# Attention and a gated two-layer product on one core: seven block products for eight in four chunks of tokens where there were two

## The chip, the core and the metric

The kernel runs on one NeuronCore of one Trainium2 chip. The core has five engines, each with an instruction queue of its own: TensorE (PE, matmuls; its weight loads are PEld), VectorE (DVE), ScalarE (ACT), GpSimd (POOL) and SyncE (SP, which here only issues DMA transfers). ACT issues a few transfers too. The metric is the device time of one execution in microseconds.

## What is computed

From the reference, with B = 8 batches, H = 8 heads, S = 576 positions, D = 64, and then 4608 tokens of 512 features and 2048 hidden units:

```python
q_d = q.reshape(B, H, Sd, factor, D).mean(axis=3)        # factor = 4; k_d, v_d alike
out_d = sm_attn(q_d, k_d, v_d)                            # softmax attention over 144 pooled positions
out_up = np.repeat(out_d, factor, axis=2)
mask = np.abs(pos[:, None] - pos[None, :]) < factor       # a band of 7 positions
scores = np.where(mask, scale * q @ k.T, -1e9)
out_local = softmax(scores) @ v
x = (out_up + out_local), heads side by side: 4608 x 512
h = x @ w_in                                              # GEMM1, 512 -> 2048
g = h * np.clip(h + 3.0, 0.0, 6.0) / 6.0
out = g @ w_out                                           # GEMM2, 2048 -> 512
```

All in fp32. The two GEMMs run in a rounded fp32 format: each operand is split into a high and a low part, and one product is three matmuls (high by high, high by low, low by high).

## The kernel before, in words

**Tokens and tiles.** The 4608 tokens are nine chunks of 512 (`PART`). One chunk's GEMM1 is 16 blocks `f` of 128 hidden units, each 4 x 3 matmuls of 128x512 into a PSUM bank `h0` or `h1` (line 1067). ACT takes relu of a block out of the bank (line 1073), DVE gates it (line 1077), ACT rounds the gated block to its high part (line 1081), DVE or POOL makes the low part (line 1085), and GEMM2 adds 4 x 3 matmuls of the block into the banks `o0` to `o3` (line 1126). At a chunk's end these four are evicted (lines 1015, 1017) and stored (line 1021).

**Attention units.** A unit is a batch and a pair of heads: 32 units, four to a batch. Batches 0 and 1 use PE for their transposes and run before and in chunk 0. For the 24 units of batches 2 to 7, PE sees one burst per unit: pooled scores and banded scores of the new unit (lines 501, 709) and the products with V of the unit that came two bursts earlier (lines 752, 664). Between them the unit's probabilities go to DRAM and come back rearranged (`put_d`, `get_d`, `put`, `get`: lines 608 to 643), and DVE transposes them in blocks of 32 (lines 631, 650). q and k come as 128-byte pieces and are transposed by DVE (lines 323, 329). The unit's result is added into `xt`, x transposed, which stays in SBUF until its chunk's split into high and low part (`plan_split`, lines 122 and 969).

**The last pair.** Chunks 7 and 8 are taken together (`plan_strassen`). Their 1024 tokens by 512 features, and two blocks of the input weights, are 2x2 block matrices, and seven products of half the depth (p1 to p7, six matmuls each, line 1370) take the place of eight. One group of seven is 42 matmuls and makes two blocks `f` for both chunks; there are eight groups. The token side needs seven matrices: b11, b21, b22 as they are and t1 to t4 as differences (line 1263), each split into high and low (line 1241). They lie where GEMM1 weights and the split x lay that no one reads any more. The weight side needs sums (lines 1333 to 1357). Products p1, p6, p7, p5 add into one bank, the "chain", which ACT copies out after p1, p6 and p7 (line 1386) before the next may add into it. The first chunk's GEMM2 runs between the products of the next group, the second chunk's GEMM2 after the last group (line 1460), from gated blocks that wait in SBUF. Twelve weight blocks are written to DRAM beforehand (line 1178) and read back (line 1321).

**What sets the order.** The program is written by a planner: each operation has costs, predecessors, buffers that it takes and frees and a latest time, and `Plan.emit` plays the kernel through and writes the instructions of each engine in the order of that play. Buffers are named slots at written-out addresses (`_slots`); most are given in a fixed turn (`ORDERED`). At run time each engine works its queue strictly in that order.

## Time and profile before

| | before |
|---|---|
| median of three runs (lowest to highest) | 905.93 us (903.33 to 907.97) |
| the profiled execution, own time | 904.18 us |
| its span, first to last instruction | 902.0 us |
| PE busy | 883.8 us (98%) |
| DVE, ACT, POOL busy | 592.2, 472.5, 237.5 us |
| DMA moved | 106.08 MB |

A row of the page's groups names the line, the engine, the operation, output <- input tiles, shape and count, then busy time, the mean of one instruction, and the idle time before the group with what ended it. The view by windows gives busy time of each engine in a stretch; DMA there is the mean busy share of the 16 DMA engines. The view in order of time gives start, length, and in brackets the idle time before an instruction. Matmuls overlap, so the length of one (0.39 us) is longer than the distance between two.

### The profile page before, as it was taken

The page shows a single profiled execution, that of the slowest core. Times are in us where ns is not written, and L with a number is a line of the kernel's source. Part 1 is how long each engine was busy: PE and PEld are TensorE (multiplying, and loading weights), DVE is VectorE, ACT ScalarE, POOL GpSimd, SP SyncE. Part 2 cuts the span into 40 slices and gives each one's busy share as a digit, 9 for nine tenths or more (in the row PEclk, how much of TensorE's full clock was granted, in tenths as well). Part 3 has the DMA queues.
Part 4 walks back from the last instruction along what each step waited for, and adds up shares of the span by engine and source line. Part 5 has one row for each costly group of instructions (what it writes and reads, how often), then busy time and mean ns, then how long its engine had stood idle before and what let it go on. Part 6 is the DMA issues. An engine that isn't in the chain of part 4 may idle for free.

```text
span 902.0 us, 19402 instructions
## 1 busy us (share of the span) xinstructions
PE 883.8 (98%) x6961; PEld 722.2 (80%) x6961; DVE 592.2 (66%) x1073; ACT 472.5 (52%) x1511; POOL 237.5 (26%) x316
## 2 busy tenths in 40 slices
PE   6999999999999999999999999999999999999997
PEld 5667788788888888888888888888888888888886
DVE  7898876466776766656666665666655868766422
ACT  5798866455655455555454535455552334444421
POOL 3655542044522132123211330223110222000000
PEclk9999999999999999999999999999999999999999
DMA  9999843366666663655365546777541022210011
GB/s 227 276 236 235 193 125 70 94 123 120 125 130 125 133 134 72 131 111 114 80 144 103 108 88 136 196 174 190 134 112 36 1 78 86 70 70 24 13 36 47
DMA packets 315759, 106.08 MB, mean 118 GB/s; under 512 B 251792, under 2 KB 298000, under 8 KB 315664
## 3 DMA queue, kind: packets, MB, share of 16 engines
q1 hardware_dynamic: 314384, 103.09, 49.7%
q10 hardware_dynamic: 1280, 1.76, 0.6%
q8 instruction: 55, 0.90, 0.4%
q14 instruction: 40, 0.33, 0.1%
HBM read 75.89 MB, written 28.90 MB: 116 GB/s over the span
## 4 chain that ended last, share of the span: by engine, by line
PE 90%; DMA 3%; DVE 2%; SPq 2%; ACT 1%; issue 0%; POOL 0%; ACTq 0%; DVEq 0%
PE o L1126 33%; PE h L1067 31%; PE o L1460 5%; PE a L1370 5%; PE h L1370 4%; PE a L1460 2%; PE h L1460 2%; PE a L709 2%; PE h L752 2%; PE a L501 1%; PE h L664 1%; DMA early<-in_v_dram 1%; DMA arena<-in_k_dram 1%; DMA out_dram<-arena 1%; SPq L323 0%; DMA arena<-in_q_dram 0%
## 5 line engine op out<-in xcount | busy, mean ns | idle before, releaser
L1126 PE MATMUL o<-wp,rounded 128*128 128x512 f32 x1344 | 324.1, 393 | 2.7 <-DVE arena L1017 1.6
L1067 PE MATMUL h<-rounded,wp 128*128 128x512 f32 x1344 | 316.9, 390 | 1.2 <-DVE arena L1077 1.0
L1067 PEld LDWEIGHTS h<-rounded,wp 128*128 128x128 f32 x1344 | 251.3, 188 | 54.8 <-DVE arena L1077 1.4
L1126 PEld LDWEIGHTS o<-wp,rounded 128*128 128x128 f32 x1344 | 249.5, 188 | 56.8 <-DVE arena L1017 2.0
L1077 DVE SCALAR_TENSOR_TENSOR arena<-arena,h 128x512 f32<-128x512 f32 x112 | 76.0, 679 | 61.8 <-ACT arena L1073 61.3
L1085 DVE TENSOR_TENSOR rounded<-arena,rounded 128x512 fp32r<-128x512 f32 x85 | 61.9, 730 | 72.0 <-PE o L1126 54.2
L1073 ACT ACTIVATE arena<-h 128x512 f32<-128x512 f32 x112 | 66.6, 594 | 78.8 <-PE h L1067 76.2
L1081 ACT CAST rounded<-arena 128x512 fp32r<-128x512 f32 x112 | 68.9, 615 | 73.9 <-PE o L1126 44.1
L565 ACT ACTIVATE arena<-arena 128x64 f32<-128x64 f32 x240 | 80.2, 337 | 0.5
L422 POOL TENSOR_TENSOR arena<-arena 32x256 f32<-32x256 f32 (+1 forms) x26 | 22.3, 858 | 117.0 <-DMA arena<-in_v_dram 116.9
L1085 POOL TENSOR_TENSOR rounded<-arena,rounded 128x512 fp32r<-128x512 f32 x27 | 35.9, 1331 | 63.9 <-PE o L1126 45.1
L329 DVE STREAM_TRANSPOSE arena<-arena 128x576 f32<-128x576 f32 x56 | 43.2, 771 | 12.7 <-DMA arena<-in_q_dram 6.3
L1460 PE MATMUL o<-wp,rounded 128*128 128x512 f32 x192 | 49.2, 389 | 0.0
L378 POOL TENSOR_TENSOR arena<-arena 128x144 f32<-128x144 f32 x33 | 14.9, 450 | 128.2 <-DVE arena L329 50.0
L565 ACT ACTIVATION_READ_ACCUMULATOR arena<-arena 128x1 f32 x240 | 45.2, 188 | 0.0
L1460 PEld LDWEIGHTS o<-wp,rounded 128*128 128x128 f32 x192 | 36.0, 188 | 7.5
L684 ACT ACTIVATE arena<-h 128x144 f32<-128x144 f32 x24 | 7.0, 290 | 66.2 <-PE h L664 66.2
L380 POOL TENSOR_TENSOR arena<-arena 128x144 f32<-128x144 f32 x66 | 38.7, 586 | 5.2
L541 ACT ACTIVATE arena<-arena 128x1 f32<-128x1 f32 (+1 forms) x78 | 15.0, 193 | 43.5 <-DVE arena L554 43.4
L1370 PE MATMUL a<-wp,wp 128*128 128x512 f32 x150 | 37.2, 389 | 0.0
L1446 DVE TENSOR_TENSOR rounded<-arena,rounded 128x512 fp32r<-128x512 f32 x27 | 18.6, 690 | 26.8 <-PE h L1460 21.1
L420 DVE TENSOR_REDUCE arena<-arena 128x128 f32<-128x512 f32 (+1 forms) x26 | 27.6, 1065 | 12.9 <-PE h L664 10.8
(240 smaller groups left out, 1239.9 us busy)
## 6 DMA issues: line engine op xcount, KB each, us to landing
rawp<-in_w_in_dram SPq DMA_DIRECT2D x16, 512.0 KB
rawp<-in_w_out_dram SPq DMA_DIRECT2D x16, 512.0 KB
arena<-in_q_dram SPq DMA_DIRECT2D x112, 72.0 KB
arena<-in_k_dram SPq DMA_DIRECT2D x112, 72.0 KB
pl<-arena SPq DMA_DIRECT2D x24, 320.0 KB
arena<-pl SPq DMA_DIRECT2D x96, 80.0 KB
arena<-in_v_dram SPq DMA_DIRECT2D x28, 256.0 KB
out_dram<-arena SPq DMA_DIRECT2D x89, 72.0 KB
```

The source lines that it names most:

```text
L329: nc.vector.transpose(out=qk[kind], in_=qk[kind])
L380: eng.tensor_tensor(t, t, x[:, :, r], op=ALU.add)
L420: eng.tensor_reduce(out=vd, in_=raw.rearrange("p r e -> p e r"), op=ALU.add, axis=AX.X)
L565: nc.scalar.activation(x[:, j], x[:, j], AF.Exp, bias=m[:, j:j + 1], scale=0.125, accum_out=s[:, j:j + 1])
L1067: nc.tensor.matmul(st["ps"], win[f][:, wt, kk * P:(kk + 1) * P], xs[part][:, kk], start=(kk == 0 and i == 0), stop=(kk == NK - 1 and i == ...
L1073: nc.scalar.activation(st["t"], st["ps"], AF.Relu, bias=3.0)
L1077: nc.vector.scalar_tensor_tensor(out=t, in0=t, scalar=6.0, in1=st["ps"], op0=ALU.min, op1=ALU.mult)
L1081: nc.scalar.copy(st["gh"], st["t"])
L1085: eng.tensor_tensor(st["gl"], st["t"], st["gh"].bitcast(F32), op=ALU.subtract)
L1126: nc.tensor.matmul(otile[n, m], gt[:, ms], wout[f][:, wt], start=(f == 0 and i == 0), stop=(f == NF - 1 and i == 2),)
L1370: nc.tensor.matmul(ps, weight(i, j, wt, kk), xpart(MOVING[j], part)[:, kk], start=first and kk == 0 and x == 0, stop=kk == half - 1 and x ...
L1460: nc.tensor.matmul(otile[n + t, m], gt[:, ms], wout[f][:, wt], start=f == 0 and x == 0, stop=f == NF - 1 and x == 2)
```

## The change

- `PAIRS = (5, 7)`: chunks 5 and 6 are a pair with seven products as well; chunks 0 to 4 stay as they were. The first pair's second GEMM2 is followed by the second pair, whose first products stand among it.
- **x by DRAM.** From batch `VIA = 2` on, a unit's x is added into one small buffer and written to DRAM by ACT's queue (`put_x`); the split of chunks 2 to 4 and the token matrices of the pairs are loaded from there (`load`, `load_x`) into the place of their own low part.
- **Gated blocks by DRAM.** In both pairs the second chunk's 16 gated blocks go to DRAM (`put_g`) and come back (`get_g`), two to three blocks ahead of their use. Both chunks of a pair now use the banks `o0` to `o3`.
- **Weights.** All 16 blocks of input weights are written to DRAM during and after chunk 0 (there were 12, around chunk 6), and 28 are read back.
- **Attention ahead.** Batches 2 to 6 must be done before the first pair starts. `due_of` gives latest times of their own, the products with V stand three bursts behind (`DEPTH`), and buffers get second places in the space that x left. q and k of two units come in one set of four transfers (`plan_qk`), the pooled probabilities in five transfers (there were eight), the tail of V in one (there were two).
- **Rules of the planner.** Operations off PE from chunk 2 on are sorted 50 us ahead (`AHEAD_BY`); a GEMM1 block gives way to a burst that waits for both `h` banks (`firm`, `yields`).

On PE, at the start of the first pair, before (a_8256 is the chain, h_8318 and h_8342 the banks of p4 and p3; one product is four to six rows, of which the first show here; "..." leaves the rest of it out):

```order
L1370 MATMUL a_8256<-wp_1213,wp_937 128x512
L1370 MATMUL a_8256<-wp_1237,wp_937 128x512
...
L1370 MATMUL h_8318<-wp_1428,wp_668 128x512
...
L1370 MATMUL a_8256<-wp_1306,wp_937 128x512
...
L1370 MATMUL h_8342<-rounded,wp_937 128x512 x2
...
L1370 MATMUL a_8256<-rounded,wp_937 128x512 x2
```

and of the change (h_6933 is the chain, first p6, then p7 from wp_1432 and p5 from wp_1205; h_7017 is p4, h_7043 p3; o_5870 is chunk 4's GEMM2):

```order
L1394 MATMUL h_6933<-rounded,wp_927 128x512 x2
...
L1173 MATMUL o_5870<-wp_1796,rounded 128x512 x3
L1394 MATMUL h_6933<-wp_1432,wp_927 128x512
L1394 MATMUL h_6933<-wp_1488,wp_927 128x512
...
L1394 MATMUL h_6933<-wp_1205,wp_927 128x512
L1394 MATMUL h_6933<-wp_1227,wp_927 128x512
...
L1394 MATMUL h_7017<-wp_1295,wp_736 128x512
...
L1394 MATMUL h_7043<-rounded,wp_927 128x512 x2
```

Before, a product into another bank stands between any two of the chain; in the change three matmuls stand between p6 and p7, and none between p7 and p5.

On ACT, at the same place of the change (L1409 copies the chain after p1, p6 and p7, L120 rounds t3, b22 and t4, L563 to L573 are a unit's softmax, L1061 evicts chunk 4's output):

```order
L1409 COPY arena<-h_6933 128x512
L563 ACTIVATE arena<-arena 128x1
L569 ACTIVATE first,arena<-a_6819,arena 128x144
L573 ACTIVATE arena<-arena 128x1
L120 CAST wp_1432<-arena 128x1024
L120 CAST rounded<-rounded 128x1024
L1409 COPY first<-h_6933 128x512
L120 CAST wp_1295<-arena 128x1024
L1061 ACTIVATE arena<-o_5797 128x512
L1061 ACTIVATE arena<-o_5870 128x512
L1409 COPY first<-h_6933 128x512
```

The rounding of t4 (wp_1295) now stands behind the copy of p6, so p4 cannot start before it.

On SP, one unit's transfers, before:

```order
L643 DMA arena<-pl_0_3840 32x20x32 x4
L616 DMA arena<-pd_0_3835 32x12x32 x4
L621 DMA arena<-pd_0_3835 32x3x16 x4
L397 DMA arena<-in_v_dram 64x4x128
L401 DMA arena<-in_v_dram 64x128
L608 DMA pd_1_4031<-arena 64x3x144 x2
L323 DMA arena<-in_q_dram 32x18x32 x4
L323 DMA arena<-in_k_dram 32x18x32 x4
L635 DMA pl_1_4077<-arena 128x5x128
```

and of the change:

```order
L638 DMA arena<-pd_1_4748 32x12x32 x5
L431 DMA arena<-in_v_dram 128x512
L435 DMA arena<-in_v_dram 32x512
L660 DMA arena<-pl_1_4873 32x20x32 x4
L422 DMA arena<-in_v_dram 64x4x128
L426 DMA arena<-in_v_dram 64x128
L630 DMA pd_2_5001<-arena 64x3x144 x2
L652 DMA pl_2_5093<-arena 128x5x128
L422 DMA arena<-in_v_dram 64x5x128
L292 DMA arena<-in_k_dram 32x36x32 x4
```

q or k of two units is now one row of four transfers, and the pooled probabilities one row of five.

The diff, cut to what the prediction speaks of:

```diff
+        if VIA <= b < WITHIN:
+            plan_qk(pair, un2, row0)
...
+        deep = DEPTH[new["un"] >= (VIA + 1, DEPTH[0])] if new else 0
+        old = next(units[0]) if len(units) >= max(deep, 1) else None
...
+    def plan_qk(pair, un, row0):
+        def get(t, kind):
+            pair[kind] = buf("qd", (kind, un), [P, 2, S])
+            raw = pair[kind].rearrange("p u (j i) -> p (u j) i", i=32)
+            for e in range(4):
+                nc.sync.dma_start(raw[32 * e:32 * e + 32], bass.AP(..., ap=[[ROW, 32], [32 * ROW, 2 * S // 32], [1, 32]]))
...
+            if b >= VIA:
+                if g == 0:
+                    st["xu"] = buf("xu", un, [P, S])
+                add_to(st["xu"][:, g * HALF:(g + 1) * HALF], g, 0, HALF)
+                return
...
+        def put_x():
+            if b not in xd:
+                xd[b] = dram.tile([P, NHP, S], F32, name=f"xd{b}", tag=f"xd{b}")
+            QUEUE[AWAY[2]](nc).dma_start(xd[b][:, hp], st["xu"])
...
+        def load(b, s0, off, cnt, k):
+            nc.sync.dma_start(part(1, k, off, cnt).bitcast(F32), xd[b][:, k:k + ks, s0:s0 + cnt])
...
+                via = [op("SP", 0.5, partial(load, b, s0, off, cnt, k), [x for h in range(k, k + ks) for x in x_done[b, h]] + gone,
+                          size=dma(P * ks, cnt * 4))] if b >= VIA else []
...
+        def load_x(name, t, kh):
+            def get(off, cnt):
+                b, s0 = divmod((n + t) * TOK + off, S)
+                nc.sync.dma_start(whole_x(name)[:, :, off:off + cnt], xd[b][:, kh * half:(kh + 1) * half, s0:s0 + cnt])
...
+        l11, l21, l12, l22 = (load_x(*x) for x in (("t1", 0, 0), ("t4", 0, 1), ("t3", 1, 0), ("t2", 1, 1)))
+        d1 = minus_x("t1", "t3", "t1", l12 + l11)
+        d2 = minus_x("t2", "t2", "t1", l22 + d1)
+        s2_ = split("t2", d2)
+        l22 = load_x("b22", 1, 1)
+        d3 = minus_x("t3", "b22", "t3", l22 + d1)
...
+                    def put_g(f=f, name=name):
+                        gs[1, f]["d"] = dram.tile([P, TOK], F32, name=f"gd{n}_{f}", tag=f"gd{n}_{f}")
+                        nc.sync.dma_start(gs[1, f]["d"], st[name])
...
+            def get_g():
+                g["t"] = {g["name"]: buf(*g["tok"], [P, TOK])}
+                nc.sync.dma_start(g["t"][g["name"]], g["d"])
...
-PAIR0, SPILL_AT, GROUP = 7, 5, 15.0
+PAIRS, GROUP = (5, 7), 15.0
+VIA, WITHIN, LATER = 2, 7, 100.0
+DUE = 170.0, 17.0, 248.0, 16.5
+SPILL_AT = 0
-DEPTH = 2
+DEPTH = 2, 3
+URGENT, AHEAD_BY = 2, 50.0
+AWAY = "SP", "SP", "ACT", "SP"
```

464 lines of the change are left out of this document (244 added, 220 removed).

## The prediction

> **What bounds the kernel now.** The page's first part and its chain of waits come first:
>
> ```profile
> PE 883.8 (98%) x6961; PEld 722.2 (80%) x6961; DVE 592.2 (66%) x1073; ACT 472.5 (52%) x1511; POOL 237.5 (26%) x316
> PE 90%; DMA 3%; DVE 2%; SPq 2%; ACT 1%; issue 0%; POOL 0%; ACTq 0%; DVEq 0%
> ```
>
> PE is busy nearly throughout and makes 90% of the chain. A busy PE need not run at its peak, so I read the distance between matmuls from the view in order of time, in chunk 8's last stretch before the pair:
>
> ```profile
> 711.55 5.60 PE L1126 MATMUL o<-wp,rounded 128*128 128x512 f32 x24
> 716.99 5.60 PE L1067 MATMUL h<-rounded,wp 128*128 128x512 f32 x24
> 722.43 5.60 PE L1126 MATMUL o<-wp,rounded 128*128 128x512 f32 x24
> 727.87 1.52 PE L1370 MATMUL a<-wp,wp 128*128 128x512 f32 x6
> ```
>
> 24 matmuls take 5.44 us from start to start, three times over: 0.2267 us each, with nothing lost between groups. The windows then say how full the rest is:
>
> ```profile
> 350.00:550.00 200.00, 200.00 (x1663) 165.95 (x1662) 126.11 (x240) 105.45 (x414) 46.34 (x76) 1.00 0.53 109
> 550.00:650.00 100.00, 100.00 (x833) 82.95 (x832) 63.36 (x121) 53.38 (x205) 21.70 (x36) 1.00 0.70 173
> 0.00:100.00 100.00, 88.84 (x990) 66.56 (x991) 86.27 (x174) 80.05 (x185) 54.40 (x61) 1.00 0.96 243
> L1067 PE MATMUL h<-rounded,wp 128*128 128x512 f32 x409 | 95.6, 389 | 0.0
> L1126 PE MATMUL o<-wp,rounded 128*128 128x512 f32 x390 | 93.5, 392 | 0.0
> L709 PE MATMUL a<-arena 64*64 64x64 f32 x320 | 7.9, 222 | 0.0
> ```
>
> A window's columns are PE, PEld, DVE, ACT, POOL, clock, DMA share and GB/s; the last three rows are PE's groups in 350 to 550. There, 799 big matmuls and 8 bursts (320 / 40) fill the 200 us: 799 x 0.2267 = 181.1, and 18.9 us for 8 bursts, 2.36 each. So a matmul taken out of this kernel is worth 0.2267 us for as long as the other engines, DMA and SP keep up. The granted clock is 1.00.
>
> **The sum, part by part.**
>
> *Products removed.* The order lists 3408 matmuls of 128x512 before and 3360 after: 8 groups x 6 = 48 fewer. 48 x 0.2267 = **10.9 us less**. Bursts and transposes on PE keep their number.
>
> *Attention run ahead.* Before, a unit has 200 / 8 = 25.0 us. In the change the 20 bursts behind chunk 1's third stand 1344 big matmuls apart in all, 67.2 each: 15.2 + 2.4 = 17.6 us per unit. Does everything else fit into that?
>
> ```profile
> L1077 DVE SCALAR_TENSOR_TENSOR arena<-arena,h 128x512 f32<-128x512 f32 x51 | 34.5, 677 | 33.6 <-ACT arena L1073 33.6
> L1085 DVE TENSOR_TENSOR rounded<-arena,rounded 128x512 fp32r<-128x512 f32 x43 | 29.7, 691 | 41.2 <-PE o L1126 29.0 <-ACT rounded L1081 12.2
> L1081 ACT CAST rounded<-arena 128x512 fp32r<-128x512 f32 x50 | 30.7, 613 | 31.0 <-PE o L1126 18.1 <-DVE arena L1077 12.9
> L1073 ACT ACTIVATE arena<-h 128x512 f32<-128x512 f32 x51 | 30.5, 597 | 36.2 <-PE h L1067 34.6
> ```
>
> These groups are from 350 to 650, 12 units. DVE works 126.11 / 8 = 15.8 us per unit, of which 64.2 / 12 = 5.4 belong to the GEMMs and shrink with the matmuls (67.2 of 99.9): 10.4 + 3.6 = 14.0 of 17.6 us, 80%. ACT: 13.2 us, 5.1 of it for the GEMMs: 8.1 + 3.4 = 11.5, 65%. DMA: 0.53 x 25.0 = 13.3 us of all 16 engines per unit. The twelve weight blocks of 512 KB, 6.3 MB, raise the share from 0.53 to 0.70 in 100 us, 17 us, or 2.7 us per MB. x written (0.295 MB per unit) and read back (5.5 MB in this stretch, 0.27 per unit) is 0.57 MB: 1.5 us. 14.8 of 17.6 is 84%; the first 100 us ran at 0.96. SP is the queue that would not have fitted:
>
> ```profile
> 403.49 2.22 SPq L323 DMA_DIRECT2D arena<-in_q_dram  x4
> 405.76 2.12 SPq L323 DMA_DIRECT2D arena<-in_k_dram  x4
> 414.85 2.78 SPq L643 DMA_DIRECT2D arena<-pl  x4
> 417.74 2.19 SPq L616 DMA_DIRECT2D arena<-pd  x4
> 420.03 1.83 SPq L621 DMA_DIRECT2D arena<-pd  x4
> ```
>
> With V and the stores to DRAM (5.1 us) a unit's issues take 16.3 us, and 0.93 of 17.6. The change issues half of q and k (2.2), five for eight of the pooled probabilities (2.5) and one V tail less (0.5): 12.1 us, 69%. ACT's 24 new issues, at some 0.5 us as on SP, are 12 us over 400. So all fit, none with much room, and SP and DVE work in order: a wait at a queue's head delays what is behind it, and on DVE that is the gate that frees an `h` bank. Below: 0. Above: every unit a tenth late on DVE's 14.0 us, less its 3.6 of room, still 0 on average, so only bunched units cost. The one wait of PE that I found beyond 100 us is this, on an eviction behind a store:
>
> ```profile
> 172.90 6.42 PE L1126 MATMUL o<-wp,rounded 128*128 128x512 f32 x27 [1.57 <-DVE arena L1017]
> ```
>
> I take 1.0, up to 5.
>
> *First pair's start.* The rows for its steps:
>
> ```profile
> 722.98 2.85 POOL L1241 TENSOR_TENSOR wp<-arena,wp 128x1024 fp32r<-128x1024 f32 x1
> 705.46 2.40 POOL L1263 TENSOR_TENSOR arena<-arena 128x1024 f32<-128x1024 f32 x1 [0.90 <-DVE arena L757]
> 705.48 3.47 DVE L1263 TENSOR_TENSOR arena<-arena 128x1024 f32<-128x1024 f32 x1
> 714.47 1.08 DVE L1263 TENSOR_TENSOR arena<-first,arena 128x896 f32<-128x896 f32 x1
> L1241 DVE TENSOR_TENSOR wp<-arena,wp 128x1024 fp32r<-128x1024 f32 x2 | 2.4, 1214 | 0.0
> L120 ACT CAST wp<-arena 128x1024 fp32r<-128x1024 f32 x2 | 2.1, 1046 | 3.6 <-DVE arena L1263 3.6
> 737.59 0.59 ACT L1386 COPY arena<-a 128x512 f32<-128x512 f32 x1 [7.57 <-PE a L1370]
> 737.39 1.52 PE L1370 MATMUL h<-wp,wp 128*128 128x512 f32 x6
> ```
>
> Let T be the end of chunk 4's last GEMM1. PE then has 45 GEMM2 matmuls and a burst, 10.2 + 2.4 = 12.6 us; p1 and p2 take 1.36 each, so p6 could start at T + 15.3, p7 at T + 17.3. t2, for p6, begins with a load into the place that this GEMM1 read. A transfer's price lies between these two pieces of the chain, a store and a load at full DMA:
>
> ```profile
> 166.37 1.82 DMA out_dram<-arena
> 31.05 4.23 DMA arena<-in_k_dram
> ```
>
> I take 3.5. Subtraction 1.2, rounding 1.05, low part on POOL 2.85, four hand-overs of 0.2 (from the rows: p6 ends at 737.39, its copy starts at 737.59): 9.4, 6 us to spare. t3, for p7: subtraction on POOL 2.4, rounding 1.05, low part 1.2, hand-overs 0.6: T + 14.7, 2.6 to spare. But t4's rounding stands behind the copy of p6 on ACT: T + 16.7 + 0.2 + 0.6, then 1.05 + 0.2 + 1.2 + 0.2 = T + 20.2, and p4 waits for it. So PE has nothing between p7 and p5 but the copy, 0.2 + 0.59 + 0.2 = 1.0, and between p6 and p7 three matmuls, 0.68, of the same 1.0. Loss: 1.0 + 0.3 = 1.3 at least. Of units still under way DVE has softmax, transposes and adds in the same 17 us; I take **2.0**, up to 7 (first rival).
>
> *Chunk 0 to 1.* Sixteen blocks of 512 KB, 8.4 MB, 22.6 us of DMA by the price above, go out between 100 and 165 us, and batch 1's last unit ends at big matmul 372 instead of 288. Behind it PE has 12 GEMM2 matmuls and part of a burst, 3.8 us, before chunk 1 begins; two adds, each no longer than the subtraction of 1.08, a rounding of 1.05, a low part of 1.2 and hand-overs of 0.6 make at most 5.0, and less with the smaller pieces there. 0 to 2; I take 0.5.
>
> ```profile
> L1017 DVE TENSOR_SCALAR arena<-o 128x512 f32<-128x512 f32 x11 | 7.6, 690 | 8.7 <-DMA out_dram<-arena 4.8 <-PE o L1126 3.9
> ```
>
> *Second GEMM2 on the banks `o0` to `o3`.* The next chunk's first product comes 9 matmuls, 2.04 us, after the bank's last; the eviction is 0.69 on DVE (the row of line 1017, x11, 690 ns) and two hand-overs, 1.1: 0. Reading gated blocks back: asked for 12 products, 8.2 us, ahead; 4.2 + 0.6 + 0.7 fit: 0. Second pair's start: its token matrices are loaded and split during the first pair's GEMM2, 16 blocks x 2.72 = 43.5 us: 0. Weights read back, 16 more: 8.4 MB over 330 us at DMA shares of 0.2: 0.
>
> Sum on the profiled execution: 904.2 - 10.9 + 1.0 + 2.0 + 0.5 = 896.8. That execution is 1.7 us below the median of its kernel's runs; with it, **898.5 us**.
>
> **Rivals.**
>
> *First: the start of the first pair starves.* POOL and DVE exclude each other: the subtraction on DVE, begun with POOL's at 705.48, took 3.47, which is POOL's 2.40 and its own 1.08. From the gate of chunk 4's fifteenth block to p2's reading, DVE's queue holds about 20 us of instructions (two low parts of weights, six large ones of tokens, a unit's reduce, transposes, adds), against 17.9 us of PE work; POOL's two large ones, 5.3 us, would come on top wherever they meet. 20 + 5.3 - 17.9 = 7.4 late at worst, 5 if a third meet nothing. For it: that row. Against it: the planner keeps the two apart, and the same start before lost nothing. 904.2 - 10.9 + 6.5 + 1.5 + 1.7 = 903, no difference that can be told. [...]
>
> *Second: nothing is lost.* Every step comes out at its lower bound, the start's 1.3 too, because t4's rounding, if p6's operands are ready early, ends while p7 runs. For it: from 190 us on nothing was lost before. Against it: p5 follows p7 in the order and needs the copy. 904.2 - 10.9 + 1.7 = 895.
>
> *Third, the other side: attention comes late.* x of batch 6 must be on DRAM before the first pair. If a unit needs more than 17.6 us, PE runs out of chunks 1 to 4 and waits, all 20 units long.
>
> ```profile
> DMA packets 315759, 106.08 MB, mean 118 GB/s; under 512 B 251792, under 2 KB 298000, under 8 KB 315664
> 181.00:237.00 56.00, 56.00 (x571) 46.52 (x562) 36.83 (x73) 32.03 (x142) 22.16 (x32) 1.00 0.63 126
> ```
>
> For it: 84% of DMA, 80% of DVE, with 251792 packets under 512 B, and weights that share the queue at the start. Against it: the second row. A burst has 108 matmuls ((1663 - 799) / 8), so 571 in 56 us are 3.3 bursts and 212 big ones (3.3 x 2.36 + 212 x 0.2267 = 55.9): units 17 us apart, with PE busy for all of it. But those were three, and twenty follow each other now. From 898.5 the sum is back at 905.9 with 7.4 us lost, 0.37 per unit. At 18.4 us a unit 16 are lost: 914; at 19 (DMA held at 0.78 of its time) 28: 926.
>
> That the change doesn't do what it says is excluded: the order has the 48 fewer.
>
> **Chances and range.** Forecast 0.52, second rival 0.22, first 0.14, third 0.12. About 0.5%, 4.5 us, is what a measurement can tell from no change: faster is below 901.4, slower above 910.5. Forecast and second rival are faster: 0.74; the first is the same: 0.14; the third slower: 0.12. The likeliest case's own range, from 1.3 to 5.5 lost, is 896 to 901. The range for 8 in 10 takes in the second rival below and the first above, with its unknown costs: 893 to 908.
>
> **What would show it.** Big matmuls stay 0.2267 us apart from 250 us to the end, in windows of chunks 1 to 4 a burst every 17.6 us; PE shows idle of 1 us before p5 and 0.3 before p7 of the first group, released by ACT's copy; DVE at 80% and DMA near 0.84 in chunks 1 to 4; the second pair's start without a gap. PE idle before p1 or p6, released by DVE or POOL, is the first rival; idle before p1 released by DMA, or GEMM1 waiting for a split, the third. What would make it wrong is loss spread over chunks 1 to 4 that no row of a slower pace shows.

## The result, and the profile after

| | before | change |
|---|---|---|
| median (lowest to highest), 15 runs each | 903.14 us (901.97 to 909.41) | 909.9 us (906.02 to 915.09) |
| profiled execution, own time / span | 904.18 / 902.0 us | 906.27 / 904.5 us |
| distance to the kernel before | | ratio 1.0068, 95% interval 1.0051 to 1.0086 |

The change made the kernel slower by 0.7%. The forecast was 898.5 us, the range 893 to 908: wrong in sign, and outside the range.

From the page of the change, the busy time of the engines, the chain of waits and the DMA traffic:

```profile
PE 878.1 (97%) x6912; PEld 712.6 (79%) x6912; DVE 636.7 (70%) x1137; ACT 497.8 (55%) x1549; POOL 268.7 (30%) x315
PE 84%; DMA 4%; DVE 3%; ACT 3%; SPq 3%; POOL 1%; issue 1%; ACTq 0%; DVEq 0%; POOLq 0%
DMA packets 338017, 151.25 MB, mean 167 GB/s; under 512 B 252288, under 2 KB 305664, under 8 KB 337920
```

PE records 49 matmuls fewer (48 by the order), but the span is 2.5 us longer, so PE stands still for longer. PE's share of the chain fell from 90% to 84%. The windows say where; their columns are, as before, PE, PEld, DVE, ACT, POOL, clock, DMA share and GB/s. The first row is of the kernel before, the others of the change:

```profile
190.00:560.00 370.00, 369.83 (x3190) 306.55 (x3189) 238.31 (x447) 196.01 (x775) 103.04 (x157) 1.00 0.57 117
190.00:560.00 370.00, 360.99 (x3580) 296.69 (x3579) 267.66 (x508) 218.74 (x918) 123.48 (x169) 1.00 0.79 167
350.00:450.00 100.00, 97.71 (x919) 80.82 (x918) 71.24 (x134) 57.01 (x235) 26.03 (x37) 1.00 0.76 158
450.00:550.00 100.00, 94.98 (x901) 77.24 (x900) 75.95 (x146) 58.72 (x253) 33.68 (x45) 1.00 0.80 176
550.00:650.00 100.00, 96.53 (x655) 77.49 (x654) 79.90 (x128) 52.63 (x124) 48.85 (x44) 1.00 0.59 167
```

In these 370 us PE idled for 0.2 us before and 9.0 us after. No engine is full there: DVE 267.66 / 370 = 72%, ACT 59%, DMA 0.79. So no engine is full in the mean, and single waits must make the loss. The view of PE's waits between 190 and 600 us (waited for; total, times, longest) has one row for the kernel before, the first one here, and nine for the change, of which the seven longest follow:

```profile
PE h L1067 <- DVE arena L757: 0.2, 1, 0.2
...
PE h L1113 <- DVE arena L1123: 3.3, 2, 2.3
PE h L1394 <- DVE first L1427: 1.9, 1, 1.9
PE h L1113 <- DVE first L774: 1.8, 2, 1.5
PE h L1394 <- ACT first L1409: 1.6, 2, 0.8
PE o L1173 <- ACT arena L1061: 1.6, 1, 1.6
PE o L1173 <- ACT rounded L1127: 1.3, 1, 1.3
PE o L1173 <- DVE rounded L1131: 0.5, 1, 0.5
```

Line 1113 is GEMM1, 1173 the first GEMM2, 1394 the seven products. Counted as a loss (the distance between two matmuls less the 0.2267 us that it has without a wait; waits of 0.25 us or more), the places are these; # is the number of big matmuls (128x512) that went before, and chunks begin at #384, 768, 1152, 1536 and 1920:

| place | loss, us |
|---|---|
| #792 and #795, behind a burst at the start of chunk 2 | 0.28, 1.66 |
| #1176, chunk 3's start | 2.45 |
| #1578, #1581, #1605, around a burst at chunk 4's start | 1.62, 0.48, 0.56 |
| #1680, #1682 and #1728 | 1.43, 0.64, 1.16 |
| first pair, before p7, p5 and p3 | 1.02, 0.92, 2.02 |
| second pair | 0.44 |

That is 14.7 us from 190 us on, where before there was 0.33.

**The balance of the two profiles.** Matmul #384 starts at 148.80 us (before: 151.46), the last one at 899.18 (896.29). So the change is 2.7 us ahead at chunk 1, takes 10.9 off, and still ends 2.9 late: it lost 16.5 us more in between. Waits of 0.25 us or more make 13.0 of that (15.05, with 0.36 at #408, against 2.06 in the kernel before), shorter ones the rest. The 2.7 us at the start are in no term of the forecast; 1.5 of them are there at the first big matmul (35.5 us against 37.1).

### The profile page after: what moved, and what is told of

The parts are those of the page before. It is cut to its first block, busy times and chain, and to the rows that moved or that the text cites. A ratio compares the mean times of both kernels' runs of the same rounds, so it can differ in the third digit from the quotient of the medians.

```text
span 904.5 us, 19378 instructions
## 1 busy us (share of the span) xinstructions
PE 878.1 (97%) x6912; PEld 712.6 (79%) x6912; DVE 636.7 (70%) x1137; ACT 497.8 (55%) x1549; POOL 268.7 (30%) x315
## 4 chain that ended last, share of the span: by engine, by line
PE 84%; DMA 4%; DVE 3%; ACT 3%; SPq 3%; POOL 1%; issue 1%; ACTq 0%; DVEq 0%; POOLq 0%
PE o L1173 22%; PE h L1113 20%; PE o L1497 19%; PE a L1394 10%; PE h L1394 7%; PE a L726 2%; DMA arena<-in_q_dram 2%; PE h L769 1%; PE a L523 1%; PE h L681 1%; DMA early<-in_v_dram 1%; DMA arena<-in_k_dram 1%; ACT arena L587 1%; SPq L1066 1%; SPq L292 1%
## 5 line engine op out<-in xcount | busy, mean ns | idle before, releaser
L1173 PE MATMUL o<-wp,rounded 128*128 128x512 f32 x960 | 234.7, 395 | 5.3 <-ACT arena L1061 1.6
L1113 PE MATMUL h<-rounded,wp 128*128 128x512 f32 x960 | 227.8, 391 | 5.5 <-DVE arena L1123 3.3
L1113 PEld LDWEIGHTS h<-rounded,wp 128*128 128x128 f32 x960 | 179.1, 188 | 45.1 <-DVE arena L1123 4.3
L1173 PEld LDWEIGHTS o<-wp,rounded 128*128 128x128 f32 x960 | 177.2, 188 | 46.0 <-ACT rounded L1127 2.3
L1497 PE MATMUL o<-wp,rounded 128*128 128x512 f32 x768 | 185.7, 390 | 0.3 <-DVE rounded L1483 0.3
L1497 PEld LDWEIGHTS o<-wp,rounded 128*128 128x128 f32 x768 | 144.0, 188 | 30.7 <-DVE rounded L1483 0.7
L1123 DVE SCALAR_TENSOR_TENSOR arena<-arena,h 128x512 f32<-128x512 f32 x80 | 54.3, 681 | 37.6 <-ACT arena L1119 37.1
L1394 PE MATMUL a<-wp,wp 128*128 128x512 f32 x306 | 76.7, 391 | 0.0
L1479 ACT CAST rounded<-arena 128x512 fp32r<-128x512 f32 x64 | 39.6, 621 | 62.9 <-PE o L1497 35.1
L1394 PEld LDWEIGHTS a<-wp,wp 128*128 128x128 f32 x306 | 57.2, 188 | 12.5 <-issue 0.4
L1127 ACT CAST rounded<-arena 128x512 fp32r<-128x512 f32 x80 | 49.1, 614 | 28.0 <-DVE arena L1123 13.4
L1394 PE MATMUL h<-wp,wp 128*128 128x512 f32 x174 | 44.0, 391 | 1.6 <-ACT first L1409 1.6
L563 ACT ACTIVATE arena<-arena 128x1 f32<-128x1 f32 (+1 forms) x78 | 15.0, 193 | 49.6 <-DVE arena L576 45.1
L1394 PEld LDWEIGHTS h<-wp,wp 128*128 128x128 f32 x174 | 32.4, 188 | 9.5 <-ACT first L1409 2.5
```

What stands on the lines that cost most here:

```text
L1113: nc.tensor.matmul(st["ps"], win[f][:, wt, kk * P:(kk + 1) * P], xs[part][:, kk], start=(kk == 0 and i == 0), stop=(kk == NK - 1 and i == ...
L1123: nc.vector.scalar_tensor_tensor(out=t, in0=t, scalar=6.0, in1=st["ps"], op0=ALU.min, op1=ALU.mult)
L1127: nc.scalar.copy(st["gh"], st["t"])
L1173: nc.tensor.matmul(otile[n, m], gt[:, ms], wout[f][:, wt], start=(f == 0 and i == 0), stop=(f == NF - 1 and i == 2),)
L1394: nc.tensor.matmul(ps, weight(i, j, wt, kk), xpart(MOVING[j], part)[:, kk], start=first and kk == 0 and x == 0, stop=kk == half - 1 and x ...
L1479: nc.scalar.copy(g["gh"], g["t"][g["name"]])
```

## The experiments

Each kernel is the change with the edit shown. Times are medians; the ratio is to the kernel before, on the same chip, with its 95% interval. The last column again counts waits of 0.25 us or more.

| run | edit in a few words | us | ratio | PE's loss behind 190 us in its profile |
|---|---|---|---|---|
| 1 | the change again | 908.23 | 1.0057 (1.0036 to 1.0077) | 13.3 |
| 2 | x's writes planned on SP | 913.15 | 1.0104 (1.0088 to 1.0120) | 18.4 |
| 3 | x's writes issued by SP, order kept | 907.06 | 1.0060 (1.0037 to 1.0084) | 14.2 |
| 4 | one pair, attention as in the change | 920.92 | 1.0197 (1.0174 to 1.0219) | 16.4 |
| 5 | one pair, attention 24 us apart | 939.35 | 1.0395 (1.0377 to 1.0414) | 34.4 |
| 6 | one pair, attention 21 us apart | 905.48 | 1.0027 (1.0012 to 1.0042) | 2.45 |
| 7 | q and k in long pieces | 905.78 | 1.0030 (1.0019 to 1.0042) | 11.8 |
| 8 | batch 7 without two transposes | 906.43 | 1.0044 (1.0028 to 1.0061) | 11.6 |
| 9 | no sums of V | 908.88 | 1.0064 (1.0049 to 1.0078) | 13.9 |
| 10 | another order by the planner's numbers | 900.75 | 0.998 (0.9967 to 0.9993) | 9.5 |
| 11 | run 10, with another time for p3 | 899.48 | 0.996 (0.9944 to 0.9975) | 7.3 |
| 12 | no burst at a chunk's start | 951.39 | 1.0528 (1.0504 to 1.0552) | 50.3 |

### 1. The change again

> The change again, on the chip of the next three. In its first trace matmuls of 128x512 lose 8.9 us beyond their 0.2267 us between 190 and 560 us, 3.5 us at the first pair's start and 1.4 us elsewhere, against 10.9 us saved. Theory A (twenty attention units packed into 67 matmuls each make transfers and the queues that issue them late, and the in-order engines behind wait): the lost time sits between 190 and 600 us again, at other places of the same stage and of another size, since it depends on when transfers land; ratio 1.005 to 1.009. Theory B (the loss is built into the order, as at the first pair's start): the same places, each within 0.3 us.

The second profile has waits at the same places: 1.66 behind #792, 1.65 at #1176, 1.63, 0.47 and 0.47 around #1578, 1.46 and 0.64 at #1680, and 1.02, 0.92 and 2.02 in the first pair. Eleven of the table's thirteen are within 0.1 us, so most of the loss is built into the order of the program. But #1176 is 0.80 us smaller, and the 1.16 at #1728 is missing. In run 8, whose program is the same up to the first pair, #1176, #1680 and #1728 are 1.49, 0.29 and 0.61. The chain of waits at these three places passes through the landing of a load of q or k, and there the size changes from one execution to the next, as the first theory had it. What a run does to one of these three must be read against that spread.

### 2 and 3. The writes of x, which ACT's queue issues

In the change's order of time, on ACT (ACTq is a transfer that ACT issues) and SP, then on PE:

```profile
349.08 1.15 ACT L120 CAST rounded<-rounded 128x384 fp32r<-128x384 f32 x2
353.16 0.33 ACTq L799 DMA_DIRECT2D xd<-first  x1
353.53 1.09 ACT L1061 ACTIVATE arena<-o 128x512 f32<-128x512 f32 x2 [3.31 <-PE o L1173]
359.80 0.57 ACT L1119 ACTIVATE arena<-h 128x512 f32<-128x512 f32 x1
346.81 5.35 SPq L292 DMA_DIRECT2D arena<-in_q_dram  x4
361.15 5.74 PE L1113 MATMUL h<-rounded,wp 128*128 128x512 f32 x24 [2.29 <-DVE arena L1123]
```

ACT does nothing from 350.23 to 353.16, although the unit's last addition was done at 349.79; then it issues the write of x (line 799). Behind it stand two evictions and a unit's softmax, and only at 359.80 the relu that starts the freeing of a bank `h`; PE waits 2.29 us for that bank. The row names DVE's gate (line 1123), which comes last, but the delay began on ACT. In the trace's semaphore events, eight counters for finished transfers serve SP's and ACT's transfers in turn; the write of x here reuses the counter of one of the four loads of q that SP issued from 346.81 on (the one of 347.37), and goes out after a wait for that counter. Over the 24 writes such waits sum to 11 us of ACT.

```diff
-AWAY = "SP", "SP", "ACT", "SP"
+AWAY = "SP", "SP", "SP", "SP"
```

> The change with x written to DRAM by SP's queue in place of ACT's; the planner orders anew. In the trace of the change x's write waited on ACT 2.9 us at 353 and 2.0 us at 489 for the landing of an earlier SP transfer that used the same completion counter, and relu of a GEMM1 block stood behind it: 2.4 and 2.1 us of PE idle. Theory C (ACT held up by this write): these waits go, 4 us less than the change. Theory A (SP and DMA packed): SP gets 0.4 us more per unit, the waits come back elsewhere, within 2 us of the change or slower.

Slower, 913.15 us, where one theory had 4 us less than the change. The planner made another order with it: the 1.43 at #1680 are gone and 1.16 stays at chunk 3's start, but the last burst before the pair comes 66 matmuls later, and the pair's start pays some 13 us. Its largest wait:

```profile
PE h L1394 <- DVE rounded L122: 6.3, 1, 6.3
```

So the run mixes two things. Run 3 keeps the order on every engine and changes the issuing queue alone:

```diff
-            QUEUE[AWAY[2]](nc).dma_start(xd[b][:, hp], st["xu"])
+            nc.sync.dma_start(xd[b][:, hp], st["xu"])
```

> The change word for word, but x's write to DRAM is issued from SP's queue, at the same place of the program, without a new plan: ACT's list loses its 24 transfers, SP's gains them, PE, DVE and POOL have the same lists. Theory C (ACT held by that write): at matmul 1176 the 1.6 to 2.4 us and at 1680 the 2.1 us fall under 0.5 each, everything else stays; total 2.5 to 4 us less than the change. Against it: SP waits at that place for the adds on DVE now, up to 3 us per unit, and its later loads come later: then these places stay or others grow, total same or more than the change.

The wait at #1176 fell to 0.59, from 1.49 to 2.45 in the three executions above: the write of x at the head of ACT's queue had made 0.9 to 1.9 us of it. The 0.26 at #1680 is no such sign, since run 8, which leaves the write on ACT, has 0.29 there; both have a piece of half clock shortly before (at 473.4 and 468.6 us). In the write's place other waits stand: 1.88 at #1800 is new, with a load of x in its chain that SP issues at 524.8 us and that lands at 530.4, and 0.90 and 1.11 are lost at #1728 and before p1 (run 7, with the write on ACT, has 1.33 before p1). The time is that of the change. ACT's share of the loss is shown at #1176 alone, and what is won there is lost elsewhere.

### 4, 5 and 6. One pair instead of two, and the room per unit

These keep x by DRAM, the weights by DRAM and the long rows of q and k, and leave chunks 5 and 6 to the normal eight products.

```diff
-PAIRS, GROUP = (5, 7), 15.0
+PAIRS, GROUP = (7,), 15.0
```

> The change with one pair (chunks 7 and 8) in seven products, everything else as in the change: x by DRAM, weights written early, attention packed to end before chunk 5. 3408 matmuls as before, so 10.9 us come back, and the first pair's start with its 3.5 us goes. Theory A (packing costs): PE still loses 7 to 12 us between 190 and 560, total 10 to 14 us above the kernel before. Rival D (the pair of chunks 5 and 6 costs it): nothing lost between 190 and 560, the time of the kernel before within 2 us.

920.92 us, 18 us above the kernel before and 4 more than the upper end of what packing was expected to cost; the pair of chunks 5 and 6 as the cause would have had nothing lost. The waits stand at the places of the change (1.65 behind #792, 2.0 at #1176, 3.1 at #1578, others between 495 and 516 us), with more between 547 and 580 us, where chunk 5 also waits for the split of its x. So the loss is there without the first pair, with attention packed to 67 big matmuls per unit. Runs 5 and 6 spread attention out as well:

```diff
-DUE = 170.0, 17.0, 248.0, 16.5
+DUE = 170.0, 24.0, 266.0, 24.0
```

> As the one with one pair, but units spread again: from big matmul 1072 (331 us in the change) on a burst every 60 to 108 matmuls, 90 in the mean, as in the kernel before; up to there as packed as in the change. x by DRAM, early weights and gated blocks by DRAM stay. Theory A: PE loses under 1 us after 331 us, at most 3 us up to there, total 1 to 4 us above the kernel before. Rival E (the moved data itself, x and weights by DRAM, costs it): the loss after 331 us stays, 8 us above the kernel before or more.

This went wrong in its own way: with units so late, x of the next chunk came late, and chunks 3 and 5 each began with one long wait for their split (9.3 and 16.0 us). It says nothing of spread units whose x is in time. Run 6 has `DUE = 165, 24, 267.9, 21` and `STAY = 7.0` (it was 6.0), with which no split is late:

> Again one pair (chunks 7 and 8), x, weights and gated blocks by DRAM, now with units spread so that no chunk waits for its x: bursts from big matmul 700 to 2080, 75 in the mean in place of 63 for the same sixteen units of the version with one pair before. Theory A' (the packed order loses): at most 4 us lost between 190 and 600 us, total 1 to 5 us above the kernel before. Rival E (the moved data itself costs it): 8 us lost there or more.

Its waits of PE from 190 to 600 us, all of them, and the window:

```profile
PE h L1113 <- DVE arena L1123: 0.7, 1, 0.7
PE o L1173 <- POOL rounded L1131: 0.5, 1, 0.5
PE h L1113 <- ACT arena L1061: 0.5, 1, 0.5
190.00:560.00 370.00, 368.20 (x3423) 303.96 (x3422) 251.58 (x476) 208.09 (x857) 122.50 (x164) 1.00 0.74 152
```

With the DMA share at 0.74 and x, weights and one pair's gated blocks by DRAM, PE loses 2.45 us, and the kernel is 0.3% (2.7 us) slower than the one before. So the data by DRAM costs at most that, where its rival asked for 8 us: it falls. Between runs 4 and 6 only `DUE` and `STAY` differ, and 15 us go: what costs is the order with attention packed, which the early start of the pair of chunks 5 and 6 asks for.

### 7. Transfers and SP

q and k of batches 2 to 6 are read in pieces of 4608 bytes in place of 128 (wrong places of the input, the same bytes).

```diff
-                    bass.AP(tensor=t.tensor, offset=t.offset + row0 * ROW + 32 * e,
-                            ap=[[ROW, 32], [32 * ROW, 2 * S // 32], [1, 32]]))
+                    bass.AP(tensor=t.tensor, offset=t.offset + (row0 + 32 * e * 9) * ROW,
+                            ap=[[9 * ROW, 32], [32, 2 * S // 32], [1, 32]]))
```

> The change with q and k of batches 2 to 6 read in rows of 4608 bytes where there were pieces of 128 bytes: the same bytes, the same number of transfers, every engine's instructions in the same order; the values land in other places, so the attention of these batches is not the reference's. It takes away what the 128-byte pieces cost the DMA engines and SP (an issue took 0.94 us in the mean). Theory F (transfers and SP late): of the six places where the change's PE idles between 190 and 560 us, the four that hang on a transfer or on SP shrink to under 0.3 us each (1.66, 1.65 to 2.45, 2.1 and 1.2 us); the one behind an eviction (2.7 us with its followers) and the first pair's start (4.0) stay: 5 to 7 us less than the change. Theory B (engines' own work in that order): all places within 0.3 us, total within 1 us of the change.

```profile
190.00:560.00 370.00, 364.89 (x3597) 300.13 (x3596) 270.55 (x512) 220.97 (x923) 124.46 (x170) 1.00 0.70 168
```

The DMA share fell from 0.79 to 0.70, SP's issue of one such transfer from 0.94 us in the mean to 0.47, SP's busy share of 190 to 560 us from 0.82 to 0.73. PE's loss fell from 13.3 and 14.7 to 11.8, and the ratio by 0.003 to 0.004: the short transfers cost 2 to 3 us (the intervals of runs 1 and 7 just overlap). Neither theory is met: 5 to 7 us or under 1 were expected, and the wait behind #792, one of four that were to go, stayed (1.58).

### 8. DVE at the first pair's start

The two transposes of pooled and banded probabilities (lines 648, 667) are left out for batch 7, whose units DVE works on while the first pair starts.

```diff
-            nc.vector.transpose(out=x, in_=x)
+            b < 7 and nc.vector.transpose(out=x, in_=x)
```

> The change without the twelve transposes on DVE of batch 7's probabilities (lines 648 and 667), whose output is then not the reference's; 1.85 us of them stand on DVE between 563 and 572 us, in the queue ahead of the instruction that frees the bank for p3 of the first group. Theory G (DVE's backlog sets that wait): p3's 2.0 us fall to 0.2, the copies' 1.0 and 0.9 us before p7 and p5 stay, everything up to 556 us stays; total 1.5 to 2.5 us less than the change. Rival H (the wait is for something else, as the earlier products): p3's wait stays over 1.5 us.

The wait before p3 was expected to go to 0.2 and only fell from 2.02 to 1.77, which was the rival's sign. The time is 1.8 us under run 1, with overlapping intervals, and part of that stands at #1680 and #1728, ahead of what was left out. In order of time, of the change: DVE's subtraction of tokens (1296) and of weights (1357) with POOL's beside them.

```profile
563.81 1.26 POOL L604 TENSOR_TENSOR arena<-arena 128x640 f32<-128x640 f32 x1
564.62 1.53 DVE L1296 TENSOR_TENSOR arena<-wp,first 128x1024 f32<-128x1024 f32 x1
570.82 1.29 POOL L1357 TENSOR_TENSOR arena<-wp 128x512 f32<-128x512 f32 x1 [5.75 <-DVE wp L1286]
572.26 0.65 DVE L1357 TENSOR_TENSOR arena<-wp 128x512 f32<-128x512 f32 x1
```

The same four without the transposes:

```profile
562.06 1.25 POOL L604 TENSOR_TENSOR arena<-arena 128x640 f32<-128x640 f32 x1
562.10 2.30 DVE L1296 TENSOR_TENSOR arena<-wp,first 128x1024 f32<-128x1024 f32 x1
569.10 1.29 POOL L1357 TENSOR_TENSOR arena<-wp 128x512 f32<-128x512 f32 x1 [5.79 <-DVE wp L1286]
569.62 1.32 DVE L1357 TENSOR_TENSOR arena<-wp 128x512 f32<-128x512 f32 x1
```

The transpose of 0.83 us had run beside POOL's addition (563.86, next to 563.81). Without it the subtraction meets that addition and takes 2.30 for 1.53; the next one takes 1.32 for 0.65. The freed time of DVE goes into waiting for POOL. This is the first rival's mechanism, at p3 instead of p1.

### 9. DVE's work per unit

The sums of V over pooled positions of batches 2 to 7 become one memset (pooled V is zero there). DVE works 248.8 us of 190 to 560 in place of 267.7, some 0.9 us less per unit, and POOL 102.0 in place of 123.5.

```diff
-            if eng is nc.vector:
-                eng.tensor_reduce(out=vd, in_=raw.rearrange("p r e -> p e r"), op=ALU.add, axis=AX.X)
+            if b >= VIA or eng is nc.vector:
+                eng.memset(vd, 0.0) if b >= VIA else eng.tensor_reduce(out=vd, in_=raw.rearrange("p r e -> p e r"), op=ALU.add, axis=AX.X)
```

> The change with the sums over four rows of V (pooled V, lines 441 to 449) of batches 2 to 7 replaced by a fill with zeros, on DVE and on POOL, so the pooled attention of these batches is not the reference's. On DVE one such sum takes 1.0 us and in three places stands ahead of the adds that free the h banks; on POOL it reads the place in which an evicted output is to land. Theory I (work of the next units, ahead in the in-order queues, holds the banks and places that PE needs at a chunk's start): at matmul 795 the 1.66 us fall to 0.6 to 0.9, at 1578 with its followers 2.6 us fall under 1.0, p3's 2.0 us at the first pair fall under 1.0 (3.3 us of DVE go ahead of it); total 3 to 5 us less than the change. Rival J (the waits have another limit right behind): each falls by less than 0.5 us, total within 1.5 us of the change.

Nothing was won: 13.9 us of loss, 1.57 at #795, 3.36 at #1176, 1.89 at #1578, 2.07 before p3. The time is that of the rival, not of the theory. What frees the banks behind a burst also runs through ACT's copies (0.27 and 0.88 us behind #792; DVE waited 0.60 for them) and a transfer's landing, so less work for DVE alone moves the limit to the next of these.

### 10 and 11. Another order of the same work

Numbers of the planner alone, nothing left out: latest times of the units, a share of DVE and POOL in some operations, and x's writes on SP.

```diff
-UNIT_T, EARLY, SLACK = (4.0, 22.0, 24.0, 24.0), 0.7, (4.0, 30.0, 50.0, 40.0)
+UNIT_T, EARLY, SLACK = (4.0, 20.4, 24.0, 24.0), 0.7, (4.0, 28.2, 50.0, 40.0)
-DUE = 170.0, 17.0, 248.0, 16.5
+DUE = 169.5, 17.0, 255.9, 16.3
-AWAY = "SP", "SP", "ACT", "SP"
+AWAY = "SP", "SP", "SP", "SP"
-STAY = 6.0
+STAY = 4.0
...
-"s512": {"DVE": 5.0}, "s256": {"DVE": 5.0}, "gl": {"POOL": 10.0}
+"s512": {"DVE": -10.0}, "s256": {"DVE": 5.0}, "gl": {"POOL": 0.0}
```

> The change with another order of the same work: x written by SP's queue, latest times of units 8 us later at the start and 0.2 us closer, and the weight sums and low parts freer between DVE and POOL. The last unit's burst stands at big matmul 1899 again, where it stood at 1966 with x on SP's queue alone. If theory C is right (ACT held by the write of x) the two places of 2.4 and 2.1 us are gone as there, and with the burst at 1899 the first pair's start costs 4 to 6 us and not 12: 4 to 7 us less than the change, 901 to 905. If x on SP's queue is what made that start late, it costs 10 us again: 909 or more.

900.75 us, just under the 901 to 905 of the theory: 0.2% faster than the kernel before, with attention packed as in the change. The waits at #1176 and #1680 are absent from this order; those behind the bursts at #792 (1.65) and #1560 (1.32) are not. Many numbers changed together, so this run shows that an order with less loss exists, not which number found it. In this order p4 already stands between p7 and p5, and the hand-over there costs nothing; the 0.69 that the next text puts before p5 is before p4. Run 11 adds one number, the time at which p3 of the first group may be placed:

```diff
-            p3 = mul(3, "p3", 12.24, [p1])
+            p3 = mul(3, "p3", 12.24 if gi else 9.0, [p1])
```

> The reordered version with one more entry changed: in the first pair's first group p3 may come ahead of p5, so that something stands between p7 and p5 while ACT copies the chain. There 0.92 us are lost before p1, 1.45 before p7, 0.69 before p5 and 1.8 in the rest of the group. If the copy is what p5 waits for, 0.7 us go and the rest stays: 0.3 to 1.5 us less than the reordered version, 899 to 900.5. If DVE is still what the group waits for, the time moves to the next product: within 0.4 us of the reordered version.

```profile
PE h L1113 <- DVE first L774: 2.6, 2, 1.5
PE h L1394 <- DMA out_dram<-arena: 1.3, 1, 1.3
PE h L1394 <- DVE arena L1427: 0.5, 1, 0.5
```

The edit did not do what that text says. PE's order is the same as in run 10 up to p5, and p3 comes later, not earlier: six matmuls of GEMM2 now stand ahead of it, and around this place the order differs on the other engines too. So the two theories on the copy were not tried, and the time within the first one's range is luck. The wait before p4 for the bank that DVE frees (line 1427) stays at 0.71, and the one before p3, 2.02 in the change and 0.34 in run 10, is gone. The start of the pair loses some 2.5 us where the change lost 4, and 7.3 us are lost in all. At 899.48 us run 11 is 0.4% faster than the kernel before; against run 10 the intervals overlap. The 48 removed products are worth having when less waits.

### 12. No burst at a chunk's start

In every order so far each wait of 1.3 to 1.7 us behind a burst in chunks 2 to 4 had three GEMM2 matmuls behind it; one burst of run 6 has six, and the loss is 0.63. From the repeat of the change:

```profile
257.19 0.97 PE L1173 MATMUL o<-wp,rounded 128*128 128x512 f32 x3
259.65 4.57 PE L1113 MATMUL h<-rounded,wp 128*128 128x512 f32 x19 [1.49 <-DVE first L774]
```

A burst takes both banks `h`; DVE's addition (line 774) frees them some 2.3 us after it. Until then PE has only GEMM2, and at a chunk's start there are three matmuls of it, 0.68 us, because GEMM2's first blocks are still being gated. All bursts of the kernel before from #396 on are followed by 12 to 24, and one of them is followed by a wait, of 0.33 us. This rule of the planner, put into its loop over PE's candidates, bars bursts from a chunk's first GEMM1 block to its third:

```diff
+                thin = e == "PE" and front[0] in (1, 2, 3, 4) and front[1] in (0, 1)
                 for _, _, o in l:
-                    if e in o.lock and locked > t + 1e-9 or kept and o.yields:
+                    if e in o.lock and locked > t + 1e-9 or kept and o.yields or thin and o.firm:
                         continue
...
+                    front = kind[:2] if kind and kind[2] == 1 else front
```

> The change with one rule more in the planner: in chunks 1 to 4 no burst of attention is placed from a chunk's first GEMM1 block until its third. Nothing is left out. By the order every burst from big matmul 484 to 1924 is now followed by 12 or more GEMM2 matmuls (before: three at 792 and at 1578), and the last burst comes at 1966 where it was at 1900. Theory K (cover): a burst holds both h banks for some 2.3 us, and GEMM1 waits when fewer than about ten GEMM2 matmuls stand behind it. Then the 1.66 us behind the burst at 792 and what is lost around the burst at 1578 (2.6 in the change) are gone, and chunks 1 to 4 lose at most 4.5 us in place of 9, with only the waits behind put_x (some 3 to 4) left. The first pair's start, whose last unit comes 66 matmuls later, loses more: 12 us with the same shift in the run with put_x on SP, where SP was late as well, so 6 to 12 here for 4.3; in all 906 to 912, no gain, which is why the bursts stand where they do. Rival L (the banks are late because DVE is late as a whole, wherever the burst stands): chunks 1 to 4 still lose 7 or more, with waits of 1 us or more behind bursts that twelve GEMM2 matmuls follow; 910 to 918.

951.39 us: both theories missed the time by more than 30. Locally the cover is right: behind all nineteen bursts from #480 to #1824 that 12 or more GEMM2 matmuls follow, the next GEMM1 waits 0.00. I had miscounted one: the 48 matmuls behind the burst at #1152 are GEMM1's own, so it has no cover at all, and PE waits 4.2 us there, for the same line. But the units that were held came late for what needs their x (waited for; total, times, longest):

```profile
PE a L523 <- POOL arena L403: 9.4, 1, 9.4
PE h L1113 <- DVE rounded L122: 9.2, 1, 9.2
PE h L1394 <- DVE rounded L122: 9.0, 1, 9.0
PE h L1113 <- DVE first L774: 4.2, 1, 4.2
```

Line 122 is the split of x: chunk 2 waits 9.2 us for its x behind #780, the first pair 9.0, and a burst 9.4 for its unit's pooled q or k (line 403). That is the third rival in full, and a reason to let bursts stand at the chunks' starts: at 67 big matmuls per unit, this rule did not keep them off the four starts without x being late. (The granted clock of this profile is 0.973, which is some of the 48 us too.)

## Why the prediction was wrong

**Right.** The removed products: 10.9 us; the dense stretches keep their pace (six matmuls in 1.36 us from 640.37 on, 0.2267 each), and behind the first pair only 0.44 us is lost, so weights and gated blocks read back, the banks `o0` to `o3` and the second pair's start cost nothing, as forecast. Chunk 0 to 1: 0.36 us for 0.5. The shares of the averages were near: DVE 72% for 80, DMA 0.79 for 0.84.

**The step that failed: "all fit, none with much room ... only bunched units cost. I take 1.0, up to 5."** Chunks 1 to 4 lost 10 us. I compared averages: work per unit against time per unit, engine by engine. None is exceeded, and still PE waits, for two reasons that averages do not hold. Run 10 packs attention as closely and loses some 4.4 us in these chunks, so more than half of the loss comes from the order of the packed work and not from its amount.
- *PE's own stock.* After a burst PE needs some 2.3 us of work that wants no bank `h`. At a chunk's start it has 0.7. With a unit each 25 us the bursts were placed elsewhere; with one each 17.6 us two of them stand there (runs 4 and 6: x and weights by DRAM with spread units lose 2.45 us; run 12: the one rule that kept them off the starts costs far more). This is about half of the 10 us, the places behind #792 and around #1578. The three quick units that I took as evidence lay outside of a chunk's start.
- *A wait at a queue's head.* "ACT's 24 new issues, at some 0.5 us as on SP, are 12 us" counted issue time only. It is 0.33 us each, but the queue stands behind a transfer whose operands or counter are not free: 2.9 us at 350 and 2.0 at 487. With what is behind it, that is 0.9 to 1.9 us of PE's loss at #1176 (run 3); at #1680 the chain of waits passes through it as well, but no run shows its share, and at #1728 DVE's queue stands behind a load of k. I wrote that such a wait delays what is behind it and then did not price one.

**SP was priced too low.** "The change issues half of q and k (2.2)": a transfer with twice the pieces took 1.8 times as long to issue (0.94 us for 0.51 in the mean), 3.25 and 5.35 us for four (below and above) where the kernel before took 2.1 to 2.2.

```profile
331.86 3.25 SPq L292 DMA_DIRECT2D arena<-in_k_dram  x4
```

Next to nothing is saved, and SP's share of 190 to 560 us went from 0.77 to 0.82 where I had 69% of a unit. Run 7, which makes the pieces long, gets 2 to 3 us; that run 3 won nothing fits a full SP, and is not shown to come from it.

**The first pair's start: 2.0 forecast, 4.0 measured.** The hand-over of the chain from p7 to p5, which I put at 1.0, lost 0.92: right. The one from p6 to p7, put at 0.3, lost 1.02:

```profile
567.01 1.04 ACT L120 CAST rounded<-rounded 128x1024 fp32r<-128x1024 f32 x1
567.96 0.57 ACT L1409 COPY first<-h 128x512 f32<-128x512 f32 x1
568.58 1.65 PE L1394 MATMUL h<-wp,wp 128*128 128x512 f32 x6 [0.85 <-ACT first L1409]
570.99 3.02 PE L1394 MATMUL h<-wp,wp 128*128 128x512 f32 x12 [0.76 <-ACT first L1409]
575.87 1.67 PE L1394 MATMUL h<-rounded,wp 128*128 128x512 f32 x6 [1.86 <-DVE first L1427]
```

p6 ended at about 567.0, just as ACT began to round b22, which stands ahead of the copy in its queue: 1.0 us that I had not counted, though the order showed it. p3 (the last row) was not in my list: I looked for late operands only, and it waits for its bank, which DVE frees late. Run 8 ties part of that to DVE and POOL excluding each other (2.30 us for 1.53 and 1.32 for 0.65 beside POOL's instructions), which the first rival had, with p1 as its place and 6.5 us as its price.

**Rivals.** The second (nothing lost) is refuted. The first had a mechanism that is at work at the start, but the wrong product and too high a price: the start lost 4.0 in all, about half of it in the chain's hand-overs. The third had the right side, but neither its signs nor its cause: in the change no GEMM1 waits for a split and p1 waits for no transfer, and run 10 fits the units into the same room. Late x appears in runs 4, 5 and 12. The text's own test holds: it was to be wrong by "loss spread over chunks 1 to 4 that no row of a slower pace shows".

**The clock.** The profile that I read had 1.00 and I left it out of the sum: a term put at nothing. Between the two profiles, both near 1.00, the change is 2.1 us slower where 7.4 us less was forecast, and the terms above make that miss. Most of the rest of the 6.8 us between the medians goes with the clock, as the last section shows.

## What to carry to other kernels

Room in the mean is not room where it is needed: when work is packed closer, look at each place where the bounding engine has a short stock of independent work (here the first two blocks of a chunk), and ask whether the packed item can still avoid it. Price an added transfer by what stands behind it in the queue of its issuer while it may not go yet (here 2.9 us on ACT at 350), and by its number of pieces as well as its count (0.94 us for 1152 pieces, 0.51 for 576). Edits that only reorder (900.75 and 899.48 us) can be worth nearly as much as the algorithm's saving, because the saving is lost in single waits of 1 to 2 us that the view of waits lists one by one.

## What the runs showed of the hardware

**Short waits were followed by half clock.** Windows of 5 us, of the change's repeat and of run 2 (clock is the third last column):

```profile
490.00:495.00 5.00, 4.24 (x19) 3.19 (x17) 3.57 (x6) 4.91 (x28) 0.00 (x0) 1.00 0.83 164
495.00:500.00 5.00, 3.99 (x12) 2.80 (x12) 4.38 (x7) 1.60 (x3) 0.72 (x1) 0.78 0.82 140
500.00:505.00 5.00, 5.00 (x119) 4.16 (x118) 2.67 (x6) 1.03 (x5) 1.24 (x3) 0.88 0.65 159
...
565.00:570.00 5.00, 1.64 (x3) 1.06 (x4) 4.96 (x6) 2.58 (x3) 2.85 (x1) 0.50 0.52 143
570.00:575.00 5.00, 4.32 (x10) 2.86 (x10) 3.82 (x4) 0.60 (x2) 0.00 (x0) 0.50 0.63 185
575.00:580.00 5.00, 5.00 (x18) 3.98 (x17) 3.17 (x2) 3.53 (x6) 3.02 (x3) 0.72 0.01 3
```

In the repeat, waits of 1.46 and 0.64 us near 495 are followed by 0.78 and 0.88: (0.22 + 0.12) x 5 = 1.7 us lost, or 3.4 us at half clock. The same piece of 3.4 us comes behind waits in runs 3, 4, 8 and 9 too. After the longer gap of run 2 (6.3 us and others) the clock is at 0.50 for 13.7 us, four such pieces.

The clock records of the traces say when it strikes. In each of the fourteen profiles all pieces at half clock begin on one grid of 3.413 us (within 2 ns); in that of the kernel before and in the first of the change the record at full clock lasts 890.879 us, 261 times 3.413, and half clock follows. Take the pieces of that grid from 190 us on, at full clock, 2908 in all, and count PE's idle time in each. All 27 with more than 1.86 us idle are followed by a piece at half clock, of the 9 with 1.65 to 1.86 us five are, and of the rest, with less, none. So in these profiles half clock came after PE stood still for about half of one such piece, in one gap or in two, and the same wait went either way by where the grid divides it: the 1.86 us before p3 in the first profile of the change fall into two pieces and cost no clock (1.00 from 575 to 580 us), in the repeat they lie in one and do (0.66).

It does not strike every execution: the first profile of the change has 1.00 in all its windows shown above, the repeat has not. Over 21 executions of the change, time falls with the mean clock by 8.6 us per 0.01 (correlation -0.86); the straight line gives 904.9 us at 1.000, and the mean clock was 0.9947. The slope is what half clock costs if PE works through it: 0.01 of a span of 905 us is 9.05 us. That PE works at half its pace there is seen in run 5: the eleven matmuls from 360.02 us, most of them at half clock, took 4.63 us, 0.42 each for 0.2267. Of the kernel before 59 executions, in the runs of the experiments, have 0.9985 in the mean and 902.4 us at 1.000 (correlation -0.40). So of the 6.6 us between the means of these executions some 2.5 are waits net of the saving, near the 2.1 between the two profiles, and about 4 the clock that follows those waits. That is a correlation over executions with the rows above as the mechanism; no run held the clock fixed.

**A transfer of 1152 small pieces holds its issuing queue about twice as long as one of long pieces.** 0.94 us in the mean (0.32 to 3.2) for 1152 pieces of 128 bytes, 0.47 for the same bytes in long pieces (run 7), but only 0.51 for 576 pieces of 128 bytes in the kernel before: it isn't in proportion to the pieces.

**A small instruction of DVE ended only with POOL's, too.** While POOL works on one of 2.39 us, this one of 32x128, which takes 0.27 us where POOL is idle (at 382.6 and 485.0), ends 0.08 us after POOL's:

```profile
559.10 2.39 POOL L1286 TENSOR_TENSOR rounded<-first,rounded 128x1024 fp32r<-128x1024 f32 x1 [1.11 <-ACT rounded L120]
559.31 2.26 DVE L449 TENSOR_SCALAR arena<-arena,head 32x128 f32<-32x128 f32 x1
```

A transpose of 128x640 with one input took its 0.83 us beside POOL (563.86 and 563.81). **What stays open:** that the shared counters alone hold ACT's writes of x was read from semaphore events and not tried by itself; how much of the loss at #1680 and #1728 is ACT's; which number of run 10 found the better order; and what, besides PE's idle time, decides between 1.65 and 1.86 us.
